# The opening of an attention and MoE kernel: its first mean square summed by TensorE in four chunks, the third weight pair rebased and half decoded earlier, and the first products of v put behind the broadcast

## The chip, the core and the metric

The kernel runs on one core of one Trainium2 chip. The metric is the device time of one execution in microseconds (us), the median of several runs. A profile is one further execution, recorded by the hardware profiler. Its times count from the first instruction that it shows. The engines are TensorE (PE, with its weight loads as PEld), VectorE (DVE), ScalarE (ACT), GpSimd (POOL) and the DMA queue that SyncE feeds (SP). Each engine works through its own list of instructions in order and waits where an operand isn't ready or a buffer isn't free.

## What is computed

Eight sequences of 576 tokens go through local attention with eight heads of 64, then through a gated feed-forward block. The reference, cut to its core:

```python
scores = q @ k.T / sqrt(64)                    # heads 0-3: the last 32 keys; heads 4-7: every 4th of the last 128
attn = softmax(where(mask, scores, -1e9))
x = (attn @ v) with the heads side by side     # 4608 tokens x 512
xn = x / sqrt(mean(x * x, axis=-1) + 1e-6) * rms_g
g, val = xn @ w_gate, xn @ w_val               # 512 -> 1536
out = (g * sigmoid(g) * val) @ w_out           # 1536 -> 512
```

All inputs and the output are float32. The weights arrive as 64-bit words (the float64 form of the values), and the kernel makes float32 of them on the chip.

## The kernel before

**Units.** The 4608 tokens are cut into 16 units of 288 (`U`). A unit's attention comes in 14 blocks: for each of four pairs of heads (`c` = 0 to 3) three or four blocks of 96 or 72 queries. A block goes through five stations: the scores on TensorE (`scored`, tile `s`), the masked maximum on VectorE (`scores_max`, two instructions, tile `t`), the exponential on ScalarE (`scores_exp`), the sum, its reciprocal and the scaling (`scores_norm`), the transposition on TensorE (`transposed`) with its copy `pt` on ScalarE, and the product with the values (`output`, tile `o`) whose copy into `xraw` is made by `take`. Then `square` squares a chunk of `xraw` on ScalarE and, in unit 0 alone, multiplies it by `rms_g` on GpSimd.

**The mean square.** Before, the squares of the four chunks are added to one tile, by GpSimd or VectorE (the function inside `square`), and `rms_sum` makes a column sum of them with six small matmuls against `inv` (1/512 in each element; tile `rps`). `rms_root` adds 1e-6 on VectorE and raises to the power of -1/2 on GpSimd (tile `rst`), `spread_first` multiplies the identity by it on VectorE (tile `rd`), `rms_apply` broadcasts it to all partitions with a matmul against ones (tile `bps`). From there ScalarE copies `root`, and VectorE multiplies the four chunks by it (`normal`, tiles `xn`).

**The feed-forward part.** For each of 12 column blocks `j`, `gate` makes the product g (four matmuls in unit 0), ScalarE its tanh, VectorE the gate `h` from both (`silu`); `val` makes the product v, and VectorE multiplies h by it (`prod`); `proj` multiplies the last h by w_out into four banks `acc`. g and v of successive j take turns in two banks of PSUM, tags "g" and "v" (`bank`): the bank that g of j+1 writes is the one in which v of j lay, so it is free once `prod` has read it. In unit 0 the first g and v (`first`, `start`) are made of the x that isn't normalized yet, by table `FIRST`, and multiplied by `root` later (tiles `g_first` and `h`).

**The weights.** They come in pairs of 128x512 pieces, 18 pairs in all (`load_pieces`, tiles `raw`, three buffers). `rebase` scales a pair's upper words into `f`, pairs 0 to 2 on GpSimd, later ones on ScalarE; from pair 4 on GpSimd also scales the upper words in place. The rest of the decoding is VectorE's: `shift`, `low` and `sign` for pairs 0 to 3, `rest` and `whole` from pair 4 on, and behind the last of them the next pair's load is issued. Pair 0 holds g and v of j = 0, pair 1 of j = 1, pair 2 w_out of j = 0 and g of j = 2, pair 3 v of j = 2 and w_out of j = 1.

**What sets the order.** The order on every engine is written out by a counter of steps (`now`). `later(dt, rank, fn)` puts a piece of work off by `dt` steps; `flush` issues the work of a step sorted by rank; then TensorE's matmuls of that step are issued by `attend`. The first 25 steps (`ends`) are the attention of unit 0. There `STEPS` says how many decode operations each step issues, `REBASES` in which steps a pair is rebased, `FIRST` where the first products stand, `ZEROS` where the upper halves of unit 1's query tiles are cleared, and `BUSY` how many matmuls on ones keep TensorE running (`busy`, five at the start, then two per step, and one in steps 17 to 19). Step 25 on belongs to the loop over `u` and `j`, three steps for a j: in it a step issues one decode operation (`decode`, two in the step `TWICE`, none in the step `PAUSE`), unit 1's blocks go along by table `SCORES`, and `split_weight` cuts the weights into a high and a low part for the later units. Once the last operation of a pair is issued, the next rebase on ScalarE follows (`begun`, `rebase_next`).

Of the kernel before, what the change touches and what calls it, by code (L numbers as in the profile page):

```python
# [9 lines left out]
F32 = mybir.dt.float32  # L10
# [4 lines left out]
ALU = mybir.AluOpType  # L15
# [5 lines left out]
P = 128  # L21
# [4 lines left out]
QB = 96  # L26
# [10 lines left out]
LAG, OUT, LATER = 4, 2, 1  # L37
STEPS = (0,) * 6 + (1, 0, 1, 0, 1) + (0,) * 2 + (1, 0, 0, 0, 1, 1) + (0,) * 4 + (2, 0)
REBASES = 5, 11, 20, 23
BUSY = 5, 2  # L40
SIGNS = 4
# [6 lines left out]
SECOND = 14, 18, 22  # L48
ZEROS = 19, 23, 26
FIRST = {19: (("g", 0), ("g", 1)), 20: (("g", 2),), 22: (("g", 3), ("v", 0), ("v", 1)),  # L50
         23: (("v", 2), ("v", 3))}

# [24 lines left out]
def attn_moe(ctx: ExitStack, tc: tile.TileContext, qk_in, v_in, w_gate, w_val, w_out, rms_g, outT):  # L77
# [82 lines left out]
    def rebase(m):  # L160
        fs[m] = cst.tile([P, 2, NC, P], F32, tag=f"slot{m}", name=f"f_{m}")


        high = raws[m][..., 1].bitcast(F32)
        if m < len(REBASES) - 1:
            G.tensor_scalar(out=fs[m], in0=high, scalar1=2.0 ** -112, scalar2=1.0, op0=ALU.mult, op1=ALU.mult)
        else:
            A.activation(out=fs[m], in_=high, func=AF.Copy, scale=2.0 ** -112)
        if m >= SIGNS:

            G.tensor_scalar(out=high, in0=high, scalar1=0.0, scalar2=1.0, op0=ALU.mult, op1=ALU.mult)
# [45 lines left out]
    def step():  # L217
        if ops:
            m, f = ops.pop(0)
            while state["rebased"] <= m:  # L220
                ahead()
            f(m)
            if (f == low and m == len(REBASES) - 1) or (f == whole and m < NP - 2):
                begun.append(m)
# [219 lines left out]
    def square(u, c):  # L444
        first = c == 0
        sq = sb.tile([P, U], F32, tag="xsq" if first else "tmp", name=f"sq_{u}_{c}", bufs=1 if first else 2)
        x = xraw[u, c]
        A.activation(out=sq, in_=x, func=AF.Square)
        if u == 0:
            G.tensor_scalar(out=x, in0=x, scalar1=gs[:, c:c + 1], scalar2=1.0, op0=ALU.mult, op1=ALU.mult)  # L450
        if first:
            xsq[u] = sq
        else:
            e = V if c == NC - 1 or u == 1 or u == 0 and c > 1 else G
            total = lambda: e.tensor_tensor(out=xsq[u], in0=xsq[u], in1=sq, op=ALU.add)
            if u == 0 and c == NC - 1:
                total()
            else:
                later(1, 0.4 if u or c < 2 else 0.55, total)

# [18 lines left out]
    def products(q, t, o, t_ps, s_tag="s", o_tag="o", wait=0):  # L479
# [50 lines left out]
        if o:  # L530
            if o[0] < NEX or wait:
                later(1, 0.5 if o[0] < NEX else 0.55, lambda: take(*o, o_ps))
            else:
                for a in range(2):
                    later(1, (0.1, 0.3)[a], lambda a=a: take(*o, o_ps, (a,)))
            if o[0] < NEX:
                later(1, 9, lambda: load_v(further(o, 3)))
            far = further(o, 2)
            if far and far[0] >= NEX:
                split_v(far, 8 if o[0] < NEX else 1)  # L540
        if q:
            later(1, 0.7, lambda: scores_max(*q, s_ps))
            behind = q == (1, 0, 2)
# [21 lines left out]
    rst = {}  # L565

    def rms_sum(u):
        r_ps = ps.tile([QB, NB, 2], F32, tag="o", name=f"rps_{u}")
        for i in range(NB):
            PE.matmul(r_ps[:, i, :], xsq[u][:, i * QB:(i + 1) * QB], inv, start=True, stop=True)  # L570
        later(1, 0.1 if u == 1 else -1.2, lambda: rms_root(u, r_ps))
        if u == 0:
            later(1, 6, spread_first)

    def rms_root(u, r_ps):
        r = sb.tile([QB, NB], F32, tag="rst", name=f"rst_{u}", bufs=2)
        V.tensor_scalar(out=r, in0=r_ps[:, :, 0], scalar1=1e-6, scalar2=None, op0=ALU.add)
        G.tensor_tensor(out=r, in0=r, in1=mhalf, op=ALU.pow)
# [91 lines left out]
    def start(kind, c):  # L670

        if kind not in first:
            first[kind] = ps.tile([P, 512], F32, tag={"g": "acc1", "v": "acc3"}[kind], name=f"{kind}_0_0")
        three(first[kind][:, :U], weight(kind, 0, 0), c, xraw[0, c], c == 0, c == NC - 1)
# [104 lines left out]
    busy_ps = ps.tile([P, 512], F32, tag="acc3", name="busy")  # L779

    def busy(n):

        for _ in range(n):
            PE.matmul(busy_ps, ones, ones[:, None, :].to_broadcast([P, 4, P]), start=True, stop=True)

# [4 lines left out]
    def plan(u, base, q_at, t_at, o_at):  # L790
# [25 lines left out]
    for n in range(ends):  # L816
# [118 lines left out]
```

## Time and profile before

| | us |
|---|---|
| median of 3 runs | 1105.61 |
| lowest, highest run | 1105.19, 1106.04 |
| the profiled execution | 1105.86 |
| its span, first to last instruction | 1104.1 |
| TensorE busy | 1095.4 (99%) |
| VectorE busy | 787.5 (71%) |
| ScalarE busy | 613.0 (56%) |
| GpSimd busy | 674.2 (61%) |

A row of the timeline has the start and the duration in us, the engine, the line of the kernel, the operation, output and inputs by the program's names, the shape, and how many instructions are merged into it. In brackets stand the idle time of the engine just ahead of the row and what ended it. [...] The granted TensorE clock is at full speed in all forty slices of the page.

### The profile page before, as it was taken

The numbers are of one execution on the slowest core, as the hardware profiler recorded it, in microseconds if no ns is written. First come the engines' busy times: TensorE is split into PE (matmuls) and PEld (weight loads), VectorE is DVE, ScalarE is ACT, GpSimd is POOL, SyncE is SP. The second block draws the span as 40 slices with busy tenths as digits, with TensorE's granted clock in tenths as the row PEclk, the third lists the DMA queues.
The fourth block names the chain that finished last, engine by engine and source line by source line (L and its number), as shares of the span: only waits on it lengthen the run. The fifth ranks groups of instructions, "written<-read, shape, count | busy, mean of one in ns | idle before, by whom it ended". The sixth has DMA issues, their size and how long they took to land.

```text
span 1104.1 us, 25573 instructions
## 1 busy us (share of the span) xinstructions
PE 1095.4 (99%) x8390; PEld 1069.8 (97%) x8390; DVE 787.5 (71%) x3097; ACT 613.0 (56%) x2200; POOL 674.2 (61%) x1153
## 2 busy tenths in 40 slices
PE   8999999999999999999999999999999999999998
PEld 6787999999999999999999999999999999999998
DVE  7889667868687676877768687686867768687412
ACT  5795676546465564646556464564646556464211
POOL 7433589756586675757657585675758657584211
PEclk9999999999999999999999999999999999999999
DMA  9775212212131131312212131131212212120000
GB/s 255 197 250 182 75 44 87 85 35 82 43 93 53 41 93 34 96 42 62 77 37 85 42 85 52 48 98 29 86 43 80 65 32 82 52 76 14 17 7 22
DMA packets 61543, 82.18 MB, mean 74 GB/s; under 512 B 7298, under 2 KB 41090, under 8 KB 61410
## 3 DMA queue, kind: packets, MB, share of 16 engines
q1 hardware_dynamic: 61410, 80.54, 24.5%
q8 instruction: 67, 1.10, 0.4%
q14 instruction: 66, 0.54, 0.2%
HBM read 71.08 MB, written 9.44 MB: 73 GB/s over the span
## 4 chain that ended last, share of the span: by engine, by line
PE 95%; ACT 1%; DVE 1%; POOL 1%; issue 1%; DMA 1%; SPq 0%; POOLq 0%; ACTq 0%; DVEq 0%
PE acc L666 17%; PE g L666 17%; PE v L666 17%; PE acc L663 9%; PE g L663 9%; PE v L663 9%; PE s L519 3%; PE o L507 3%; PE acc L660 2%; PE v L660 2%; PE g L660 2%; PE t L492 2%; PE g L492 1%; PE o L504 1%; PE s L516 1%
## 5 line engine op out<-in xcount | busy, mean ns | idle before, releaser
L733 POOL TENSOR_TENSOR hlo<-th,hhi 128x288 fp32r<-128x288 f32 x179 | 145.8, 814 | 161.3 <-ACT hhi L732 146.9
L399 ACT ACTIVATE t<-t,sum 96x128 f32<-96x128 f32 (+3 forms) x448 | 165.8, 373 | 108.9 <-DVE sum L384 106.3
L666 PE MATMUL acc<-hhi,lo 128*128 128x288 f32 x720 | 212.7, 295 | 0.0
L415 POOL TENSOR_SCALAR t<-t,sum 72x72 f32<-72x72 f32 (+3 forms) x414 | 147.8, 368 | 85.9 <-DVE sum L409 74.9
L703 ACT ACTIVATE th<-g 128x288 f32<-128x288 f32 x180 | 73.8, 410 | 194.0 <-PE g L666 99.2
L666 PE MATMUL g<-xhi,lo 128*128 128x288 f32 x612 | 180.3, 295 | 0.0
L666 PE MATMUL v<-xhi,lo 128*128 128x288 f32 x612 | 180.2, 294 | 0.0
L437 DVE TENSOR_REDUCE xraw<-o 64x72 f32<-64x144 f32 (+1 forms) x364 | 117.0, 322 | 83.9 <-PE o L507 79.5
L708 DVE SCALAR_TENSOR_TENSOR th<-th,g 128x288 f32<-128x288 f32 x180 | 80.8, 449 | 100.0 <-ACT th L703 76.1
L666 PEld LDWEIGHTS acc<-hhi,lo 128*128 128x128 f32 x720 | 135.4, 188 | 0.0
L323 POOL TENSOR_TENSOR vhl<-vt,vhl 128x128 fp32r<-128x128 f32 x182 | 84.4, 464 | 70.1 <-ACT vhl L319 66.6
L732 ACT CAST hhi<-th 128x288 fp32r<-128x288 f32 x180 | 77.7, 432 | 76.0 <-DVE th L721 75.1
L666 PEld LDWEIGHTS g<-xhi,lo 128*128 128x128 f32 x612 | 115.2, 188 | 0.0
L666 PEld LDWEIGHTS v<-xhi,lo 128*128 128x128 f32 x612 | 115.1, 188 | 0.0
L721 DVE TENSOR_TENSOR th<-th,v 128x288 f32<-128x288 f32 x180 | 79.8, 443 | 43.6 <-PE v L666 43.5
L439 DVE TENSOR_TENSOR xraw<-o,xraw 64x72 f32<-64x72 f32 (+1 forms) x364 | 101.2, 278 | 12.5
L663 PE MATMUL acc<-hhi,hi_o 128*128 128x288 f32 x360 | 109.0, 303 | 0.0
L663 PE MATMUL g<-xhi,hi_g 128*128 128x288 f32 x357 | 107.0, 300 | 0.0
L666 PE MATMUL acc<-hlo,hi_o 128*128 128x288 f32 x360 | 106.4, 296 | 0.0
L362 POOL TENSOR_TENSOR qs<-qk,qs 64x288 fp32r<-64x288 f32 x104 | 84.3, 811 | 24.5 <-ACT qs L357 17.3
L353 POOL TENSOR_TENSOR ks<-qk,ks 128x288 fp32r<-128x288 f32 (+2 forms) x104 | 97.1, 938 | 3.1
L666 PE MATMUL g<-xlo,hi_g 128*128 128x288 f32 x322 | 95.1, 295 | 0.0
(188 smaller groups left out, 3463.4 us busy)
## 6 DMA issues: line engine op xcount, KB each, us to landing
qk<-in_qk_dram SPq DMA_DIRECT2D x60, 288.0 KB, 2.8
vt<-in_v_dram SPq DMA_DIRECT2D x196, 64.0 KB, 1.9
qk<-in_qk_dram SPq DMA_DIRECT2D x30, 352.0 KB, 3.0
out_dram<-ot SPq DMA_DIRECT2D x64, 144.0 KB, 1.9
qk<-in_qk_dram SPq DMA_DIRECT2D x30, 304.0 KB, 2.8
raw<-in_w_gate_dram SPq DMA_DIRECT2D x12, 512.0 KB, 5.4
raw<-in_w_val_dram SPq DMA_DIRECT2D x12, 512.0 KB, 5.5
raw<-in_w_out_dram SPq DMA_DIRECT2D x12, 512.0 KB, 4.4
```

The lines of the kernel that those rows point to most:

```text
L323: G.tensor_tensor(out=vp[:, :, 1], in0=vs.pop(b), in1=vp[:, :, 0], op=ALU.subtract)
L353: ek.tensor_tensor(out=ks[:, 1, :nkt], in0=kr, in1=ks[:, 0, :nkt], op=ALU.subtract)
L362: eq.tensor_tensor(out=qs[D:], in0=qr[D:], in1=qs[D:], op=ALU.subtract)
L399: A.activation(out=t[:nq, a, :n], in_=t[:nq, a, :n], func=AF.Exp, scale=-1.0, bias=sm[:nq, a, 0:1], accum_out=None if by_rows(u, c, i) els ...
L415: (V if u == 0 and (c, i) > (NC - 1, 0) else G).tensor_scalar(out=t[:nq, a, :n], in0=t[:nq, a, :n], scalar1=sm[:nq, a, 3:4], scalar2=1.0, ...
L437: V.tensor_reduce(out=ours, in_=o[:D, cols:cols + 2 * nq].rearrange("d (t q) -> d q t", t=2), axis=mybir.AxisListType.X, op=ALU.add)
L439: V.tensor_tensor(out=ours, in0=o[D:, cols:cols + nq], in1=ours, op=ALU.add)
L663: PE.matmul(out, wh[:, cc, :], xh, start=start, stop=False)
L666: PE.matmul(out, w[:, cc, :], v, start=False, stop=stop and k == 1)
L708: V.scalar_tensor_tensor(out=t, in0=t, scalar=1.0, in1=g, op0=ALU.add, op1=ALU.mult)
L721: V.tensor_tensor(out=t, in0=t, in1=v_ps[:, :U], op=ALU.mult)
L733: (V if (u, j) == (NU - 1, NJ - 1) else G).tensor_tensor(out=lo, in0=t, in1=hi, op=ALU.subtract)
```

## The change

The squares of the four chunks of unit 0 are no longer added. Each chunk's square goes to TensorE by itself as soon as it is there (`part_sum`, six small matmuls each, in steps 12, 13 and 18 by the new table `SUMS` and in step 21), into 24 columns of the bank in which the dummies write. The dummies have 384 columns for that, and there are three per step for two (seven at the start for five), none in the steps with a sum or a first product. VectorE adds up the four sums with one reduction (`rms_root`). Three additions of squares go: one on GpSimd, two on VectorE.

The tables: pair 2 is rebased in step 16, not 20, and its shift and low stand in steps 19 and 20, its sign in step 24; before, shift and low stood in step 23 and the sign in step 25. The rest of the decoding moves up by one operation, and with it ScalarE's rebases from pair 4 on: `begun` is set behind the shift of pair 3, not behind its low. In the first products one chunk of v stands ahead of the broadcast and three behind it, two and two before, and v lies in the bank "acc0". The maxima of unit 1's first scores and the spread change places by rank, the copies of o stand ahead of the exponentials of the same step (rank 0.41), and unit 1's tiles are cleared later.

The diff, cut to its core:

```diff
-STEPS = (0,) * 6 + (1, 0, 1, 0, 1) + (0,) * 2 + (1, 0, 0, 0, 1, 1) + (0,) * 4 + (2, 0)
-REBASES = 5, 11, 20, 23
+STEPS = (0,) * 6 + (1, 0, 1, 0, 1) + (0,) * 2 + (1, 0, 0, 0, 1, 1, 1, 1, 0, 0, 0, 1)
+REBASES = 5, 11, 16, 23
...
-            if (f == low and m == len(REBASES) - 1) or (f == whole and m < NP - 2):
+            if (f == shift and m == len(REBASES) - 1) or (f == whole and m < NP - 2):
...
         if u == 0:
             G.tensor_scalar(out=x, in0=x, scalar1=gs[:, c:c + 1], scalar2=1.0, op0=ALU.mult, op1=ALU.mult)
-        if first:
+        if u == 0:
+            squares.append(sq)
+        elif first:
             xsq[u] = sq
...
-                later(1, 0.5 if o[0] < NEX else 0.55, lambda: take(*o, o_ps))
+                later(1, 0.41 if o[0] < NEX else 0.55, lambda: take(*o, o_ps))
...
-            later(1, 0.7, lambda: scores_max(*q, s_ps))
+            later(2 if q == (1, 0, 0) else 1, 0.6 if q == (1, 0, 0) else 0.7, lambda: scores_max(*q, s_ps))
...
+    def part_sum(c):
+        for i in range(NB):
+            PE.matmul(sum_ps[:, c, i, :], squares[c][:, i * QB:(i + 1) * QB], inv, start=True, stop=True)
+
     def rms_sum(u):
+        if u == 0:
+            part_sum(NC - 1)
+            later(1, -1.2, lambda: rms_root(u, sum_ps))
+            later(1, 0.65, spread_first)
+            return
...
-        V.tensor_scalar(out=r, in0=r_ps[:, :, 0], scalar1=1e-6, scalar2=None, op0=ALU.add)
+        total = r_ps[:, :, 0]
+        if u == 0:
+            V.tensor_reduce(out=r, in_=r_ps[..., 0].rearrange("q c i -> q i c"), axis=mybir.AxisListType.X, op=ALU.add)
+            total = r
+        V.tensor_scalar(out=r, in0=total, scalar1=1e-6, scalar2=None, op0=ALU.add)
...
+    sum_ps = busy_ps[:QB, 3 * P:3 * P + 2 * NB * NC].rearrange("q (c i t) -> q c i t", c=NC, t=2)
...
-            PE.matmul(busy_ps, ones, ones[:, None, :].to_broadcast([P, 4, P]), start=True, stop=True)
+            PE.matmul(busy_ps[:, :3 * P], ones, ones[:, None, :].to_broadcast([P, 3, P]), start=True, stop=True)
...
-        if n < nb + LAG + OUT:
+        if n in SUMS:
+            part_sum(SUMS.index(n))
+        elif n < nb + LAG + OUT and n not in FIRST:
             busy(0 if n < 2 else BUSY[1] if n < nb + LAG - 1 else 1)
```

Where the instructions stand. On TensorE, from the first product on; g_0_0 and v_0_0 are the first products, s_1 are scores of unit 1, a product's second input is the weight pair. Before:

```order
L660 MATMUL g_0_0_528<-xraw_0_0_255,f_0_215 128x288
L660 MATMUL g_0_0_528<-xraw_0_1_329,f_0_215 128x288
L516 MATMUL s_1_0_0_534<-qk_1_0_115 96x128 x2
L660 MATMUL g_0_0_528<-xraw_0_2_411,f_0_215 128x288
L516 MATMUL s_1_0_1_545<-qk_1_0_115 96x128 x2
L570 MATMUL rps_0_556<-inv_73,sq_0_0_334 96x2 x3
L660 MATMUL g_0_0_528<-xraw_0_3_493,f_0_215 128x288
L660 MATMUL v_0_0_561<-xraw_0_0_255,f_0_215 128x288
L660 MATMUL v_0_0_561<-xraw_0_1_329,f_0_215 128x288
L516 MATMUL s_1_0_2_579<-qk_1_0_115 96x128 x2
L612 MATMUL bps_0_582<-rd_0_572,ones32_99 128x288
L660 MATMUL v_0_0_561<-xraw_0_2_411,f_0_215 128x288
```

In the change, at the same place:

```order
L670 MATMUL g_0_0_545<-xraw_0_0_262,f_0_220 128x288
L670 MATMUL g_0_0_545<-xraw_0_1_339,f_0_220 128x288
L515 MATMUL s_1_0_0_550<-qk_1_0_115 96x128 x2
L568 MATMUL busy_146<-inv_73,sq_0_3_553 96x2 x3
L515 MATMUL s_1_0_1_559<-qk_1_0_115 96x128 x2
L670 MATMUL g_0_0_545<-xraw_0_2_424,f_0_220 128x288
L670 MATMUL g_0_0_545<-xraw_0_3_511,f_0_220 128x288
L670 MATMUL v_0_0_583<-xraw_0_0_262,f_0_220 128x288
L515 MATMUL s_1_0_2_591<-qk_1_0_115 96x128 x2
L622 MATMUL bps_0_594<-rd_0_571,ones32_99 128x288
L670 MATMUL v_0_0_583<-xraw_0_1_339,f_0_220 128x288
L670 MATMUL v_0_0_583<-xraw_0_2_424,f_0_220 128x288
```

The sum is the last chunk's alone and stands one product and one block of scores earlier, the products with chunks 2 and 3 follow it together, and one product of v has gone from ahead of bps to behind it.

On ScalarE, from the first tanh (h_0) on; f_4 is the rebase of pair 4, xraw_1_0 the copy of unit 1's first o, rows with a sum as an output are exponentials. Before:

```order
L703 ACTIVATE h_0_608<-g_first_609 128x288
L472 COPY pt_1_0_0_625<-t_0_0_620 128x192
L399 ACTIVATE t_1_0_2_600,sum1_87<-t_1_0_2_600,sum1_87 96x128 x2
L399 ACTIVATE t_1_1_0_612,sum2_88<-t_1_1_0_612,sum2_88 96x128 x2
L412 ACTIVATE t_1_0_2_600<-t_1_0_2_600,sum1_87 96x128 x2
L703 ACTIVATE h_1_650<-g_0_1_636 128x288
L472 COPY pt_1_0_1_652<-g_0_1_636 128x192
L168 ACTIVATE f_4_659<-raw_4_521 128x1024
L412 ACTIVATE t_1_1_0_612<-t_1_1_0_612,sum2_88 96x128 x2
L399 ACTIVATE t_1_1_1_654,sum3_89<-t_1_1_1_654,sum3_89 96x128 x2
L433 COPY xraw_1_0_677<-o_1_0_0_668 64x96 x2
```

In the change, at the same place:

```order
L713 ACTIVATE h_0_624<-g_first_625 128x288
L169 ACTIVATE f_4_633<-raw_4_539 128x1024
L471 COPY pt_1_0_0_644<-t_0_0_639 128x192
L401 ACTIVATE t_1_0_2_613,sum1_87<-t_1_0_2_613,sum1_87 96x128 x2
L401 ACTIVATE t_1_1_0_628,sum2_88<-t_1_1_0_628,sum2_88 96x128 x2
L414 ACTIVATE t_1_0_2_613<-t_1_0_2_613,sum1_87 96x128 x2
L713 ACTIVATE h_1_669<-g_0_1_655 128x288
L471 COPY pt_1_0_1_671<-g_0_1_655 128x192
L414 ACTIVATE t_1_1_0_628<-t_1_1_0_628,sum2_88 96x128 x2
L435 COPY xraw_1_0_694<-o_1_0_0_687 64x96 x2
L401 ACTIVATE t_1_1_1_673,sum3_89<-t_1_1_1_673,sum3_89 96x128 x2
```

The rebase of pair 4 has moved up by six rows, and the copy of o stands ahead of the last exponentials.

On VectorE, up to the product of h_2 with v; raw_4, f_4 are rest and whole of pair 4, raw_5 and f_5 of pair 5, rows with a mask are maxima. Before:

```order
L252 TENSOR_TENSOR lo_0_688<-f_0_215,hi0_g0_687 128x512
L186 SCALAR_TENSOR_TENSOR raw_4_521<-raw_4_521 128x1024
L190 SCALAR_TENSOR_TENSOR f_4_659<-f_4_659,raw_4_521 128x1024
L408 TENSOR_REDUCE sum4_90<-sum4_90 96x2
L409 RECIPROCAL sum4_90<-sum4_90 96x2
L384 ISA t_1_2_0_735,sum0_86<-s_1_2_0_722,mask_77 72x104
L384 ISA sum0_86 72x1
L384 ISA t_1_2_0_735,sum0_86<-s_1_2_0_722,mask_77 72x104
L384 ISA sum0_86 72x1
L708 SCALAR_TENSOR_TENSOR h_2_731<-h_2_731,g_0_2_717 128x288
L186 SCALAR_TENSOR_TENSOR raw_5_617<-raw_5_617 128x1024
L721 TENSOR_TENSOR h_2_731<-h_2_731,v_0_2_743 128x288
```

In the change, the rows up to the same product:

```order
L253 TENSOR_TENSOR lo_0_703<-f_0_220,hi0_g0_702 128x512
L187 SCALAR_TENSOR_TENSOR raw_5_636<-raw_5_636 128x1024
L410 TENSOR_REDUCE sum4_90<-sum4_90 96x2
L411 RECIPROCAL sum4_90<-sum4_90 96x2
L386 ISA t_1_2_0_754,sum0_86<-s_1_2_0_741,mask_77 72x104
L386 ISA sum0_86 72x1
L386 ISA t_1_2_0_754,sum0_86<-s_1_2_0_741,mask_77 72x104
L386 ISA sum0_86 72x1
L718 SCALAR_TENSOR_TENSOR h_2_750<-h_2_750,g_0_2_736 128x288
L191 SCALAR_TENSOR_TENSOR f_5_732<-f_5_732,raw_5_636 128x1024
L731 TENSOR_TENSOR h_2_750<-h_2_750,v_0_2_765 128x288
```

One decode operation more is done ahead of the product: whole of pair 5 stands where its rest stood. It is the same ahead of the product of h_1, where the sign of pair 3 stands for its low.

On VectorE around the root, the four decode operations f_1 low, f_1 sign, f_2 shift and f_2 low follow each other with nothing between, then come the reduction, the addition of 1e-6, the maxima of the first scores and the spread; before, the two additions of squares stood among them, and shift and low of pair 2 came behind the root. The sign of pair 2 now stands ahead of g_first, before it stood behind h_0's gate. On GpSimd the rebase of pair 2 stands between the scalings of chunks 1 and 2, in the place of the addition of squares; before, it stood between those of chunks 2 and 3, behind two clearings of unit 1's tiles. The order of SP's queue changes only from pair 13's load on, around 75 us of the trace before.

More of the change, by code (lines that the diff above doesn't have):

```diff
@@ L37 @@
 LAG, OUT, LATER = 4, 2, 1
-STEPS = (0,) * 6 + (1, 0, 1, 0, 1) + (0,) * 2 + (1, 0, 0, 0, 1, 1) + (0,) * 4 + (2, 0)
-REBASES = 5, 11, 20, 23
-BUSY = 5, 2
+STEPS = (0,) * 6 + (1, 0, 1, 0, 1) + (0,) * 2 + (1, 0, 0, 0, 1, 1, 1, 1, 0, 0, 0, 1)
+REBASES = 5, 11, 16, 23
+BUSY = 7, 3
+SUMS = 12, 13, 18
 SIGNS = 4
@@ L48 @@
 SECOND = 14, 18, 22
-ZEROS = 19, 23, 26
-FIRST = {19: (("g", 0), ("g", 1)), 20: (("g", 2),), 22: (("g", 3), ("v", 0), ("v", 1)),
-         23: (("v", 2), ("v", 3))}
+ZEROS = 22, 24, 26
+FIRST = {19: (("g", 0), ("g", 1)), 21: (("g", 2), ("g", 3)), 22: (("v", 0),),
+         23: (("v", 1), ("v", 2), ("v", 3))}
 SCORES = {1: (-3, -2, 0, 1, 3, 4, 6, 7, 9, 10, 12, 13, 15, 16),
@@ L164, in rebase @@
         high = raws[m][..., 1].bitcast(F32)
-        if m < len(REBASES) - 1:
+        if m < 3:
             G.tensor_scalar(out=fs[m], in0=high, scalar1=2.0 ** -112, scalar2=1.0, op0=ALU.mult, op1=ALU.mult)
@@ L370, in attn_moe @@
     st, xraw, xsq = {}, {}, {}
+    squares = []
     def scores_max(u, c, i, s_ps):
@@ L450, in square @@
             G.tensor_scalar(out=x, in0=x, scalar1=gs[:, c:c + 1], scalar2=1.0, op0=ALU.mult, op1=ALU.mult)
-        if first:
+        if u == 0:
+            squares.append(sq)
+        elif first:
             xsq[u] = sq
         else:
[L454 to L459, printed above, removed]
+            later(1, 0.4, lambda: (V if c == NC - 1 or u == 1 else G).tensor_tensor(out=xsq[u], in0=xsq[u], in1=sq, op=ALU.add))
     def bursts(u):
@@ L571, in rms_sum @@
         later(1, 0.1 if u == 1 else -1.2, lambda: rms_root(u, r_ps))
-        if u == 0:
-            later(1, 6, spread_first)
     def rms_root(u, r_ps):
         r = sb.tile([QB, NB], F32, tag="rst", name=f"rst_{u}", bufs=2)
-        V.tensor_scalar(out=r, in0=r_ps[:, :, 0], scalar1=1e-6, scalar2=None, op0=ALU.add)
+        total = r_ps[:, :, 0]
[3 more added lines that the diff above has]
+        V.tensor_scalar(out=r, in0=total, scalar1=1e-6, scalar2=None, op0=ALU.add)
         G.tensor_tensor(out=r, in0=r, in1=mhalf, op=ALU.pow)
@@ L672, in start @@
         if kind not in first:
-            first[kind] = ps.tile([P, 512], F32, tag={"g": "acc1", "v": "acc3"}[kind], name=f"{kind}_0_0")
+            first[kind] = ps.tile([P, 512], F32, tag={"g": "acc1", "v": "acc0"}[kind], name=f"{kind}_0_0")
         three(first[kind][:, :U], weight(kind, 0, 0), c, xraw[0, c], c == 0, c == NC - 1)
@@ L794, in plan @@
         last = base + (o_at[-1] if u < NNAT else DONE)
-        events.setdefault(last + (4 if u == 1 else 3), {})["sum"] = u
+        events.setdefault(last + (2, 4, 3)[min(u, 2)], {})["sum"] = u
         events.setdefault(last + (4, 7, 5)[min(u, 2)], {})["apply"] = u
@@ L799, in attend @@
         e = events.pop(now[0], {})
+        if e.get("sum") == 0:
+            rms_sum(e.pop("sum"))
         if any(k in e for k in "qto"):
```

## The prediction

> **What bounds the kernel now.** I read the page's first line, then the view of who waited for whom, for TensorE alone and over the whole run, then the timeline of TensorE across the opening; the last line of the fence is a row of the chain of waits.
>
> ```profile
> span 1104.1 us, 25573 instructions
> ...
> PE busy L784 <- ACT ones L94: 2.4, 1, 2.4
> PE o L504 <- ACT xraw L433: 1.5, 2, 1.3
> PE t_first L492 <- POOL t L415: 0.7, 2, 0.5
> PE g L660 <- POOL xraw L450: 0.4, 1, 0.4
> ...
> 29.81 1.13 PE L660 MATMUL g<-xraw,f 128*128 128x288 f32 x4
> 30.78 0.60 PE L516 MATMUL s<-qk 128*96 128x128 f32 x4
> 31.22 0.65 PE L660 MATMUL g<-xraw,f 128*128 128x288 f32 x2
> ...
> 33.15 0.75 PE L660 MATMUL g<-xraw,f 128*128 128x288 f32 x2 [0.41 <-POOL xraw L450]
> ...
> 35.14 0.72 PE L612 MATMUL bps<-rd,ones 96*128 96x288 f32 x2
> 35.70 1.14 PE L660 MATMUL v<-xraw,f 128*128 128x288 f32 x4
> ...
> 37.28 2.13 PE L660 MATMUL g<-xn,f 128*128 128x288 f32 x8
> ...
> 46.11 0.59 PE L504 MATMUL o<-pt,v 128*128 128x192 f32 x2 [1.28 <-ACT xraw L433]
> 46.54 2.10 PE L660 MATMUL g<-xn,f 128*128 128x288 f32 x8
> ...
> 54.13 2.10 PE L660 MATMUL g<-xn,f 128*128 128x288 f32 x8
> ...
> 97.55 0.43 PE rps L570 x6
> ```
>
> The four groups are all the waits that TensorE has in 1104.1 us. Of the second group only 0.2 us is left behind the wait at 46.11; otherwise TensorE runs without a gap to the end, so nothing that makes another engine faster later can shorten the span. What the change wins it must win ahead of the row at 46.54, the product g_0_2, and it keeps that only if no new wait appears behind. What can go is 0.41 us ahead of 33.15, 1.28 us ahead of 46.11, and dummies on the path. Each row begins with its issue; from one start to the next is what it costs its engine.
>
> **The change part by part.** *Dummies and sums.* Six sum matmuls cost 0.43 (last row), a pair of scores 0.44 (30.78 to 31.22), two g matmuls 0.97 (29.81 to 30.78). Ahead of the first products one dummy goes, one becomes a sum and one is shorter; in the earlier steps 1152 dummy columns stand for 1024, and two steps have a sum instead. TensorE waits for other engines between these, so I count the gain at nothing where the sum of columns alone would say 0.3, and keep 0.3 either way.
>
> *The rebase of pair 2, moved ahead on GpSimd.* It stands where an addition of squares stood.
>
> ```profile
> 23.89 1.23 DVE L415 TENSOR_SCALAR t<-t,sum 72x72 f32<-72x72 f32 x2
> 27.11 1.22 DVE L177 SCALAR_TENSOR_TENSOR f<-raw,f 128x1024 uint32<-128x1024 uint32 x1
> 28.25 0.45 DVE L455 TENSOR_TENSOR sq<-sq,sq 128x288 f32<-128x288 f32 x1
> 28.61 1.22 DVE L181 SCALAR_TENSOR_TENSOR f<-raw,f 128x1024 uint32<-128x1024 uint32 x1
> 33.11 0.67 DVE L174 TENSOR_SCALAR f<-f 128x1024 uint32<-128x1024 uint32 x1
> ...
> 24.10 0.79 POOL L455 TENSOR_TENSOR sq<-sq,sq 128x288 f32<-128x288 f32 x1
> 27.99 2.21 POOL L450 TENSOR_SCALAR xraw<-xraw,gs 128x288 f32<-128x288 f32 x1 [3.11 <-ACT sq L448]
> 31.49 1.12 POOL L166 TENSOR_SCALAR f<-raw 128x1024 f32<-128x1024 f32 x1
> 32.58 0.51 POOL L450 TENSOR_SCALAR xraw<-xraw,gs 128x288 f32<-128x288 f32 x1
> 33.05 1.46 POOL L578 TENSOR_TENSOR rst<-rst,mhalf 96x3 f32<-96x3 f32 x1
> 99.14 0.87 POOL L578 TENSOR_TENSOR rst<-rst,mhalf 96x3 f32<-96x3 f32 x1 [1.81 <-DVE rst L577]
> ```
>
> Two small normalizations on VectorE took 1.23 us from 23.89 on: they stood until GpSimd's addition was over at 24.10 + 0.79 = 24.89. GpSimd in turn took 2.21 us for a scaling that takes 0.51 at 32.58: it stood through three VectorE instructions in a row, to 28.61 + 1.22 = 29.83. So each shuts the other out. A rebase of 1.12 where the addition of 0.79 stood makes VectorE's normalizations, and TensorE's transposes behind them, 0.33 later. That I set against the dummies, and let the first product start at 29.81 again.
>
> VectorE then runs four decode steps in one piece: low and sign of pair 1, shift and low of pair 2. A big one costs 1.14 (27.11 to 28.25), a shift 0.6 (its 0.67 less the same overlap): 27.11 + 0.33 + 1.14 + 1.14 + 0.6 + 1.14 = 31.46. By the row at 27.99 GpSimd stands all that time, and its two scalings end at 31.9 and 32.4. TensorE asks for them at 29.81 + 0.97 + 0.44 + 0.43 + 0.44 = 32.09 and 32.57: just in time, and the wait of 0.41 goes. The power on the sums follows at 32.4. It took 1.46 beside the shift at 33.11, and 0.87 at 99.14; no decode step stands beside it now, so 33.3, and the spread (rd, the size of the addition at 28.25, 0.45) is there at 33.75.
>
> TensorE comes to the broadcast (bps) at 32.09 + 0.97 + 0.49 + 0.44 = 33.99, behind rd: no wait, and 35.14 before. Then bps 0.56, three products 1.46, scores 0.44, transposes 0.17 (as before in sum): the first product on the normalized x starts at **36.6, 0.7 us earlier** than 37.28.
>
> [...]
>
> *Behind the broadcast.*
>
> ```profile
> 36.32 1.52 DVE L623 TENSOR_TENSOR xn<-xraw,bps 128x288 f32<-128x288 f32 x4
> 38.31 0.46 DVE L702 TENSOR_TENSOR g_first<-g,root 128x288 f32<-128x288 f32 x1
> 44.81 0.44 DVE L721 TENSOR_TENSOR h<-h,v 128x288 f32<-128x288 f32 x1
> 46.86 0.14 DVE L408 TENSOR_REDUCE sum<-sum 96x2 f32<-96x4 f32 x1
> ...
> 47.12 0.67 DVE L252 TENSOR_TENSOR lo<-f,hi_g 128x512 fp32r<-128x512 f32 x1
> 51.87 1.23 DVE L186 SCALAR_TENSOR_TENSOR raw<-raw 128x1024 uint32<-128x1024 uint32 x1 [0.70 <-POOL raw L171]
> 53.01 0.45 DVE L721 TENSOR_TENSOR h<-h,v 128x288 f32<-128x288 f32 x1
> 55.15 1.34 DVE L252 TENSOR_TENSOR lo<-f,hi_g 128x512 fp32r<-128x512 f32 x1
> ...
> 38.80 0.44 ACT L703 ACTIVATE h<-g_first 128x288 f32<-128x288 f32 x1
> 52.88 1.17 ACT L168 ACTIVATE f<-raw 128x1024 f32<-128x1024 f32 x1
> ...
> 54.13 1.83 POOL L171 TENSOR_SCALAR raw<-raw 128x1024 f32<-128x1024 f32 x1 [2.30 <-ACT f L168]
> ```
>
> From xn's end (37.84) to g_first (38.31) VectorE has one block's maxima, 0.47; a sum with its reciprocal costs 0.26 (46.86 to 47.12); an instruction on 128x288 costs 0.36 (28.25 to 28.61). Ahead of xn VectorE now takes the second block's maxima and, once ScalarE has its two exponentials (at most 0.44 each, the tanh's row being longer), its sum: 33.75 + 0.47 + 0.85 + 0.26 = 35.3, against 36.32. But the sign of pair 2 (1.14) now stands ahead of g_first, which it followed before: 35.3 + 1.52 + 0.47 + 1.14 = 38.4 where 38.31 stood. The tanh is 0.49 behind that, at 38.8 to 38.9. Of xn's 1.0 us nothing is left here.
>
> ScalarE now rebases pair 4 (1.17, by 52.88) right behind that tanh, no longer ahead of the copy of o that TensorE waited for at 46.11; the exponentials ahead of that copy go behind it, too. What is left ahead is a scaling that waits for VectorE's second sum, 43.5 below, and two small ones: the copy is done by 44.6. TensorE asks at 36.6 + 7.55 (37.28 to 46.11 without the wait) = 44.2: **the wait of 1.28 shrinks to some 0.4**.
>
> *What is late next.* The bank that g_0_2 writes is free when VectorE has multiplied h_1 with v. That ended at 44.81 + 0.37 = 45.18, in time for 46.54 less 1.28. In the changed order one more decode step (sign of pair 3) stands ahead of it. From the tanh at 38.8: gate 39.2, shift 39.6, product 40.2, h times root 40.5. Meanwhile ScalarE's rebase ends at 40.4, and GpSimd's scaling of pair 4 (1.12) starts beside the product, which reads PSUM. h times root has both operands in SBUF, as the subtraction at 55.15 has, which took 1.34 against 0.67 at 47.12 while GpSimd's scaling of 54.13 ran to 55.96. So h times root ends at 41.8. Undisturbed, the sum behind it would still wait for ScalarE's exponentials, to 41.1. From there sum 0.26, low 1.14, sum 0.26 (43.5), maxima 0.47, gate 0.36, sign 1.14, product 0.36 make 4.0: 45.8, or 45.1. TensorE wants g_0_2 at 44.6. So g_0_2 starts at **45.8 (or 45.1), 0.7 (or 1.4) us earlier** than before, held by VectorE.
>
> The next product, h_2 with v, began 8.2 us after that one (44.81 to 53.01) with four big decode steps between and a wait of 0.70 for GpSimd's scaling of pair 5. In the changed order there are four again and the same scaling, behind a longer piece of VectorE's; I leave 8.2. It ends at 54.0 (or 53.3) and frees g_0_3's bank, which TensorE took at 54.13, 0.75 behind the product: there **0.1 (or 0.8)** of the gain is left. I take 0.3, nearer to the disturbed end, which has a row. Further on the order within a j is as before, and 0.3 is less than the 0.75 of cover in the row that was tightest in the opening, so I carry it to the end.
>
> *A second wait, just hidden.* Pair 6's rebase moves one step ahead on ScalarE, ahead of a copy of o, while its load still waits for the sign of pair 3.
>
> ```profile
> 47.00 0.33 SPq L154 DMA_DIRECT2D raw<-in_w_val_dram  x1
> ...
> DMA to landing us min/median/max: 3.2/5.2/7.8
> ```
>
> The loads issue at 45.4 and 45.8 now. Before, the rebase at 52.88 came 5.9 behind 47.00 without a wait, so the pair has landed by 51.3; rebase 1.17 and 1.0 of scaling and copy make 53.5 where TensorE asks at 45.8 + 7.2 = 53.0. g_0_3 behind it would start at 53.9, and the product holds it to 54.0 anyway.
>
> **Sum.** The profiled execution took 1105.86 us, the span of 1104.1 and 1.8 around it; less 0.3 it is 1105.6. It stands 0.25 above the median of the runs, 1105.61, whose forecast is **1105.3**. A measurement of this kernel can tell some 0.2% (2.2 us) from no change.
>
> **Rivals.** *TensorE's own order is the bound.* If VectorE's products are never late, 0.7 + 1.28 stays: 1103.6. For it speaks that I add many small pieces; against it that 0.75 us of cover was left at 53.38 and the gain must fit in. Chance 0.20.
>
> *The broadcast doesn't come earlier, against what the change says.* If GpSimd is shut out over 1.1 us longer than reckoned, bps stays at 35.1 while the sign of pair 2 now delays g_first: VectorE's chain is 1.2 later than above and g_0_3 starts at 55.2, 1.1 late: 1106.7. The 2.21 row speaks for it; against it, VectorE has little to run behind 31.46. Chance 0.14.
>
> *Slower: ScalarE stands at pair 6's rebase.* At the longest landing, 7.8 us, the load is there at 53.6, the copy done at 55.8, g_0_3 starts at 56.2, 2.1 late: 1107.7. It decides from a landing of 5.6 us on. Chance 0.10.
>
> **How the numbers follow.** The forecast has 0.56, with a range of its own from 1104.8 (0.8 gained) to 1105.5. The range goes down to the first rival and up to the second, 1103.6 to 1106.7; outside lie the third and the tails. Faster by over 0.2% needs more than all waits named: 0.06. Slower by over 0.2% needs the longest landing and a little: 0.06. Within: 0.88.
>
> **What will show it.** Right: no wait ahead of the last g_0_0 product, bps near 34.0, the first product on xn near 36.6, and in TensorE's list of waits a VectorE product (h from h and v) ahead of g where the copy of o stood. Wrong: TensorE without any wait from 37 to 60; a wait for a copy of o near 53; bps at 35 or later; the wait of 1.28 still there.

## The result, and the profile after

The changed kernel is slower. The median of its nine runs is 1111.83 us, beside 1105.86 for nine runs of the kernel before on the same chip: a ratio of 1.0053, 95% interval 1.0034 to 1.0073. The forecast was 1105.3 with a range up to 1106.7, so the time lies outside it, and on the other side.

The single runs say more than the median, because they come in steps, and the steps go with TensorE's mean granted clock: 1107.56 and 1107.59 at a clock of 1.000, 1109.12 at 0.998, 1110.98 at 0.997, 1111.83 at 0.995, and 1114.11 to 1114.86 at 0.992. The kernel before had 1.000 in the profile that the prediction read. So there are two losses: some **1.7 us at full clock** (1107.57 against 1105.86), and **0 to 7 us that come with the clock**, in the median run 4.3. Two single executions far off all others, 1514 us of run 8 and 3778 us of the kernel before, are left out of every median and count below.

The profiled execution is the run of 1110.98, its span 1109.2 against 1104.1. The view of who waited for whom, for TensorE (engine, tile and line; what it waited for; us in total, times, longest):

```profile
PE busy L796 <- ACT ones L95: 2.4, 1, 2.4
PE s L515 <- DVE sum L386: 1.4, 1, 1.4
PE t_first L491 <- POOL t L417: 1.3, 2, 0.9
PE v L670 <- ACT pt L471: 0.6, 1, 0.6
PE t_first L491 <- DVE t L417: 0.3, 1, 0.3
PE o L503 <- ACT xraw L435: 0.2, 1, 0.2
PE bps L622 <- ACT rd L606: 0.2, 1, 0.2
```

The two waits that the prediction wanted gone are gone: nothing waits for a GpSimd scaling ahead of g, and the 1.28 us for the copy of o is gone (the 0.2 is the second wait of that group, there before). In their place stand 1.4 us for VectorE's maxima (s, the scores) and 0.6 us for a copy of pt (v, a value product), and the transposes t_first wait 1.6 us in the opening where they waited 0.7. All waits together are 6.4 us where they were 5.0: 1.4 of the 5.1 us that the span grew. The rest is in no list of waits. It is in the granted clock, which the windows view shows; its columns are the stretch and its length, TensorE's busy time with its instructions, the granted clock, the share of the DMA engines and GB/s:

```profile
core 0: us, PE busy (x), PEclk, DMA share, GB/s
30.50:31.00 0.50, 0.50 (x5) 1.00 0.46 101
31.00:31.50 0.50, 0.50 (x3) 0.57 0.12 33
...
37.00:37.50 0.50, 0.50 (x3) 0.50 1.09 173
37.50:38.00 0.50, 0.50 (x3) 0.61 0.77 109
```

In the rows not shown the clock is 1.00 or 0.50 and nothing between, so a half microsecond at 0.57 was at full clock for 14% of it: the clock fell at 31.07, and by the row at 0.61 it rose at 37.89. That is 6.8 us at half clock, 3.4 us lost, which is what lies between this run and those at 1.000, and, with the 1.4 of waits, nearly all that the span grew. TensorE's busy time doesn't show it: it is 0.50 of 0.50 throughout. What shows it is the timeline, where the same instructions take nearly twice as long:

```profile
21.28 0.77 PE L796 MATMUL busy<-ones 128*128 128x384 f32 x3
...
22.70 0.61 PE L568 MATMUL busy<-inv,sq 128*96 128x2 f32 x6
...
24.03 0.61 PE L568 MATMUL busy<-inv,sq 128*96 128x2 f32 x6
...
25.01 0.79 PE L796 MATMUL busy<-ones 128*128 128x384 f32 x3
...
30.69 1.95 PE L670 MATMUL g<-xraw,f 128*128 128x288 f32 x4
...
35.10 2.13 PE L670 MATMUL g<-xraw,f 128*128 128x288 f32 x4
...
38.38 0.65 PE L622 MATMUL bps<-rd,ones 96*128 96x288 f32 x2
```

The first four matmuls of g (two products, each with two matmuls in the profile) took 1.13 us in the kernel before; here they take 1.95, as the clock falls 0.38 us behind their start, and the next four, at half clock throughout, take 2.13. The broadcast starts at 38.38, where 33.99 was forecast, and ahead of that, between the dummies that end at 21.89 and those at 25.01, TensorE had 3.1 us of small products only: transposes, scores and value products on 72 columns, and the sums, which stand where dummies stood.

### The profile page after: what moved, and what is told of

The parts are those of the page before. It is cut to its first block, busy times and chain, and to the rows that moved or that the text cites. A ratio compares the mean times of both kernels' runs of the same rounds, so it can differ in the third digit from the quotient of the medians.

```text
span 1109.2 us, 25625 instructions
## 1 busy us (share of the span) xinstructions
PE 1099.1 (99%) x8417; PEld 1074.8 (97%) x8417; DVE 783.1 (71%) x3096; ACT 613.6 (55%) x2200; POOL 670.4 (60%) x1152
## 4 chain that ended last, share of the span: by engine, by line
PE 92%; DVE 2%; POOL 2%; ACT 2%; DMA 1%; issue 1%; SPq 0%; POOLq 0%; DVEq 0%; ACTq 0%
PE acc L676 17%; PE v L676 17%; PE g L676 17%; PE acc L673 9%; PE v L673 9%; PE g L673 8%; PE o L506 3%; PE s L518 3%; PE t L491 2%; PE g L670 1%; PE acc L670 1%; PE v L670 1%; PE s L515 1%; PE g L491 1%; DMA raw<-in_w_val_dram 1%
```

## The experiments

Three theories for the clock: **C**, the dummies that the sums displaced; **W**, TensorE's new short waits; **D**, the dummies' 384 columns in place of 512. For the 1.7 us at full clock: **V**, the decode that runs one step ahead, against **S**, the sums themselves. "The clock fell" below means a mean clock of 0.998 or less; as an estimate, that is at least some 3.3 us at half clock in a span of 1105 (0.998 is rounded from 0.9985 at most, 0.15% of the span is 1.66 us, and at half clock half of the time is lost). A mean of 0.999 isn't counted: in the profile of the kernel before the clock goes down behind TensorE's last product as well, where nothing is lost. That product's row is at 1100.42, and between 1103.5 and 1104.0 the clock is 0.87 with TensorE busy for 0.00 us. Each group of four ran on one chip beside runs of the kernel before, whose medians were 1105.59, 1105.80 and 1105.81.

### 1. All dummies back

```diff
         if n in SUMS:
             part_sum(SUMS.index(n))
-        elif n < nb + LAG + OUT and n not in FIRST:
+        if n < nb + LAG + OUT:
             busy(...)
```

> The changed kernel, with the dummies of steps 12, 13, 18 and 19 issued besides the sums. Theory C (clock): the dummies taken out where the sums stand let the granted clock fall to half for a time that differs from run to run, 0 to 7 us lost. Then all runs here have a clock of 1.000 and lie close together, at 1107.6 (the changed kernel's best runs) plus up to 1.9 for the dummies' own time on TensorE: 1107.6 to 1109.5, no run above 1110. Rival W (waits): the clock falls because TensorE waits (0.94 at 13.63, 0.35 at 26.14), which this edit leaves: runs still spread up to 1114 with clocks down to 0.992. Rival D (narrow dummies): the clock falls because the dummies have 384 columns in place of 512: still spread, too.

Measured: 1108.41 to 1108.90 in six runs, clock 0.999 to 1.000 in all; ratio 1.0028 (1.0017 to 1.0040). The steps are gone. The dummies are still the narrow ones, so D falls, and the waits of 0.7 and 1.4 us behind the opening are there, too. W isn't settled by this run: the wait of 0.35 at 26.14 is gone from its profile, too, as the dummies fill it. The loss at full clock stays.

### 2. The kernel before without four steps' dummies

```diff
-        if n < nb + LAG + OUT:
+        if n < nb + LAG + OUT and n not in (12, 13, 18, 19):
             busy(...)
```

> The kernel before, without the dummies of steps 12, 13, 18 and 19 (two, two, one and one), and nothing else changed; no part of the result is left out. Theory C: the clock falls below 1.000 in some or all runs, with times from 1105.3 to 1113. Rival W and rival D: clock 1.000 in all runs and 1105.0 to 1106.0, since the waits and the width of the other dummies are those of before.

Measured: median 1107.52 (1105.53 to 1108.42), ratio 1.0015 (1.0006 to 1.0023); the clock fell in 8 of 11 runs, to 0.995. So taking the dummies away does it without anything else of the change. The profile is of a run at full clock, so it doesn't show where the clock fell in the others.

### 3. The changed kernel with the old decode

```diff
-STEPS = (0,) * 6 + (1, 0, 1, 0, 1) + (0,) * 2 + (1, 0, 0, 0, 1, 1, 1, 1, 0, 0, 0, 1)
-REBASES = 5, 11, 16, 23
+STEPS = (0,) * 6 + (1, 0, 1, 0, 1) + (0,) * 2 + (1, 0, 0, 0, 1, 1) + (0,) * 4 + (2, 0)
+REBASES = 5, 11, 20, 23
...
-            if (f == shift and m == len(REBASES) - 1) or (f == whole and m < NP - 2):
+            if (f == low and m == len(REBASES) - 1) or (f == whole and m < NP - 2):
```

> The changed kernel with the decode steps and the rebase of the third pair where they were before. Theory C: the clock falls as in the changed kernel (0.992 to 1.000, a spread of several us). For the 1.7 us that the changed kernel's best runs lose at full clock: theory V (VectorE and GpSimd collisions from the moved decode) says that the best runs here come back to 1105 to 1106.3; rival S (the sums and the order of the products cost it) says that they stay at 1107 to 1108.

Measured: 1104.78 to 1105.86 in the four runs at clock 1.000, and up to 1114.92 (clock 0.989) in the others; ratio 1.0026 (1.0006 to 1.0045). At full clock the loss of 1.7 is gone: theory V. The parts of the edit go together here; runs 7, 8 and 11 separate the opening from what comes behind it. The profile is of a run at 0.997, and it speaks plainly on the clock. The windows view, with the columns as above:

```profile
26.00:28.00 2.00, 2.00 (x20) 1.00 1.01 193
28.00:30.00 2.00, 2.00 (x17) 0.82 0.87 171
30.00:32.00 2.00, 2.00 (x10) 0.50 0.96 276
```

TensorE was busy 2.00 of 2.00 in each of these, and in the three stretches ahead of them from 20 on; its timeline names no idle time from 22 to 60. So no wait in the 9 us ahead of the fall lowered this clock, and W falls as the cause here: a TensorE that by its records never rests can still lose its clock. Half clock isn't always paid in full either: this run had 6.8 us of it, 3.4 us lost by the sum above, and its 1106.58 is only 0.7 to 1.8 us above the four at full clock.

### 4. The kernel before with the new decode

The same lines the other way round, in the kernel before.

> The kernel before with only the rebase and decode steps of the third pair moved ahead. Theory C: clock 1.000 in all runs, for all dummies are there. Theory V: 1107 to 1108, the 1.7 us that the changed kernel loses at full clock. Rival S: within 0.5 of the kernel before, 1105.3 to 1106.4.

Measured: 1110.71 to 1112.01 in five runs, clock 0.995 to 0.997 in all; ratio 1.0052 (1.0040 to 1.0064). I had expected a full clock, since no dummy is missing. None of the five is at full clock, so the times say nothing of V against S; but the list of waits has, with no sums by chunks in the kernel, the two that V needs:

```profile
PE s L516 <- DVE sum L384: 1.4, 1, 1.4
PE v L660 <- ACT pt L472: 1.1, 1, 1.1
```

The timeline has a long wait ahead of the fall; VectorE, GpSimd, then TensorE, and the windows:

```profile
23.64 2.30 DVE L415 TENSOR_SCALAR t<-t,sum 72x72 f32<-72x72 f32 x2
...
23.86 0.80 POOL L455 TENSOR_TENSOR sq<-sq,sq 128x288 f32<-128x288 f32 x1
24.64 1.09 POOL L166 TENSOR_SCALAR f<-raw 128x1024 f32<-128x1024 f32 x1
...
25.92 0.33 PE L492 MATMUL t_first<-ident,t 72*72 72x72 f32 x2 [1.09 <-DVE t L415]
...
24.00:26.00 2.00, 0.91 (x8) 1.00 1.03 152
26.00:28.00 2.00, 2.00 (x14) 0.70 1.04 222
```

In this kernel GpSimd has the addition of squares and the rebase, and VectorE's two normalizations stand through both: 2.30 us. TensorE waits 1.09 and was busy 0.91 of 2.00 us between 24 and 26; the clock fell at 26.8, by the row at 0.70. So theory W isn't wrong everywhere: a long wait in the opening goes with a lower clock, too, though no run here took that wait away alone. In the changed kernel, which has no addition there, the wait is 0.35, and run 3, which has none, loses its clock as well.

### 5 and 6. Which dummies: the late two steps or the early two

Both stand on run 3, the changed kernel with the old decode, which has no waits of its own.

```diff
-        elif n < nb + LAG + OUT and n not in FIRST:
+        if n < nb + LAG + OUT and n not in (12, 13):      # run 5
+        if n < nb + LAG + OUT and n not in (18, 19):      # run 6
```

> The changed kernel with the old places of the third pair's decode, and the dummies of steps 18 and 19 back, those of 12 and 13 left out. Theory L (late): the clock falls because the last steps ahead of the first products have small products only; in both profiles of kernels without those dummies it fell 0.4 to 0.7 us behind the first product's start. Then clock 1.000 in all runs, 1105.2 to 1106.2 (1105.5, the full-clock runs without the dummies, and up to 0.7 for these). Theory E (early): steps 12 and 13 count as much; the clock still falls in about half of the runs, up to 1115.

> The counterpart of the run before: the dummies of steps 12 and 13 back, those of 18 and 19 left out. Theory L: the clock still falls in half of the runs, 1105.5 to 1112. Theory E: clock 1.000, 1105.5 to 1106.8.

Measured: with the late dummies (5) the clock still fell in 5 of 12 runs, to 0.992; 1105.68 to 1113.10, ratio 1.0014 (1.0001 to 1.0027). With the early ones (6) it was 1.000 in all 11; 1106.49 to 1107.73, ratio 1.0008 (1.0000 to 1.0017). My theory L fell (and the fall in the two profiles that it named came 0.38 and 0.34 us behind the first product's start, 31.07 after 30.69 and 29.27 after 28.93, not 0.4 to 0.7). **The dummies of steps 12 and 13 hold the clock**, the two steps in which the sums displaced the dummies in the middle of small transposes and scores. Whether it is their place or their number isn't shown: run 6 gives back six dummies, three in each step, and run 5 two, one in each. Run 6 is also 1.4 us above the kernel before in its median, over the range expected, with a wait of 0.64 for a copy of o in its profile; the old decode isn't free of waits once these dummies are back. The profile of run 5 has the fall where this says it should be, right behind those steps. The timeline, then the windows:

```profile
21.79 0.62 PE L568 MATMUL busy<-inv,sq 128*96 128x2 f32 x6
23.12 0.61 PE L568 MATMUL busy<-inv,sq 128*96 128x2 f32 x6
24.09 0.98 PE L796 MATMUL busy<-ones 128*128 128x384 f32 x3
```

```profile
24.00:24.50 0.50, 0.50 (x6) 1.00 1.11 201
24.50:25.00 0.50, 0.50 (x5) 0.51 0.99 167
...
41.50:42.00 0.50, 0.50 (x4) 0.92 0.00 0
```

From 24.51 to 41.58 it stayed at half: 17.1 us.

### 7 and 8. The wait for pt and the wait for the maxima

On run 1, with all dummies. Run 7 has the first line, run 8 both.

```diff
-            if (f == shift and m == len(REBASES) - 1) or (f == whole and m < NP - 2):
+            if (f == low and m == len(REBASES) - 1) or (f == whole and m < NP - 2):
...
-                    decode((t != PAUSE) + (t == TWICE))
+                    decode((t not in (2, PAUSE)) + (t == TWICE))
```

> The changed kernel with all four steps' dummies back (1108.7 at full clock), and in it ScalarE's rebase of the fifth pair one step later again: behind the fourth pair's low part, as before, and no longer behind its shift. The wait of 0.65 for pt ahead of a value product goes. Theory P (waits add up): 1108.0. Theory Q (VectorE's decode, one step ahead, sets the scores' maxima, for which TensorE waits 1.38 at 53.3): TensorE only comes earlier to that wait, which grows to about 2.0, and the time stays at 1108.5 to 1108.8.

> As the run before, and the decode besides pauses for one step behind the opening, so that from there on every decode step stands where it stood in the kernel before; only the third pair's sign stays ahead of the gate. Theory Q: both waits (0.65 and 1.38) go, 1106.4 to 1107.0. Rival R: the moved work in the opening is what costs, and the time stays above 1108.

Measured: run 7 median 1108.14 (1107.30 to 1109.96), ratio 1.0020 (1.0011 to 1.0029): the wait of 0.7 for pt is gone, that of 1.38 for the maxima stands at the same size, and doesn't grow, as Q had it. Against the kernel before on its own chip run 7 loses 2.3 us and run 1 lost 3.1, 0.8 less, about the wait of 0.7, which speaks for P. The clock fell in 1 of 10 runs (0.998). Run 8 median 1105.84 (1105.51 to 1112.01), ratio 1.0006 (0.9995 to 1.0017), the clock down in 1 of 11 (0.995): with the decode put back to its old steps behind the opening, both waits are gone and so is the loss. That is below the range expected. Rival R is out: what was moved ahead in the opening costs nothing that can be measured; what costs is that every later decode step then also comes one step ahead.

### 9 to 12. The early dummies alone, and what is left

Run 9 is the changed kernel with the dummies of steps 12 and 13 alone. Run 10 adds `PAUSE, TWICE = 31, 5` (before 31, 6); run 11 instead adds both lines of run 8; run 12 is run 11 with one dummy in steps 12 and 13 in place of three.

> The changed kernel with the dummies of steps 12 and 13 alone back, beside the sums there. Theory E (these two steps hold the clock): clock 1.000 in all runs and 1107.4 to 1108.4, that is, what the changed kernel takes in its runs at full clock (1107.6) and at most 0.7 more. Rival: with the new decode order TensorE has short waits in the opening, which the old order doesn't have, and the clock still falls in some runs (1109 to 1114).

> As the run before, with the one step that decodes two pieces also put one step earlier, so that the rest of pair 5 no longer stands in the same step as the whole of pair 4. Theory Q2: this order alone makes VectorE wait for GpSimd's scaling of pair 5 and TensorE for the maxima behind it (1.38); that wait goes, the one of 0.65 for pt stays, and the time is 1.0 to 1.4 below the run before, 1106.3 to 1107.0. Rival: the pieces only queue up elsewhere, within 0.4 of the run before.

> The changed kernel with the dummies of steps 12 and 13 back, the fifth pair's rebase behind the low part, and the decode paused for one step behind the opening: sums by chunks, third pair's sign ahead, no new wait. If the waits and the clock are the whole loss, this is within 0.6 of the kernel before on either side, and its best runs 0.3 to 0.6 below it, 1104.9 to 1105.9. If the sums or the moved sign cost something of their own: 1106.3 or more.

> As the run before with one dummy in steps 12 and 13 in place of three each. If the clock asks for no more than a little dense work between the small products: clock 1.000 and up to 0.8 less than the run before. If it goes by the amount of dense work: the clock falls in some runs, up to 1112.

Measured: run 9 median 1108.65 (1107.93 to 1109.80), ratio 1.0026 (1.0017 to 1.0034), the clock fell in 1 of 11 runs (0.998): the two steps' dummies hold the clock with the new decode, too; the median is some 0.3 us over the range expected. Run 10 median 1108.61, ratio 1.0027 (1.0018 to 1.0036), the clock down in 1 of 11 (0.995): no gain, the wait for the maxima is 1.5; Q2 fell, it isn't the double step but the order as a whole. Run 11 median 1105.91, ratio 1.0002 (0.9994 to 1.0011), the clock down to 0.997 in 2 of 11. Run 12: eight of 11 runs between 1104.58 and 1105.51 at full clock, three with the clock down and 1108.22 to 1111.44; ratio 1.0003 (0.9989 to 1.0016). Against run 11's 2 of 11, 3 of 11 doesn't tell whether one dummy a step is too little. None of them beats the kernel before by more than can be measured.

Run 9 is the changed kernel's own order at full clock, and so shows the waits undisturbed. Two rows of its list of waits, then the timelines of TensorE, VectorE and ScalarE:

```profile
PE s L515 <- DVE sum L386: 1.7, 2, 1.4
PE v L670 <- ACT pt L471: 0.7, 1, 0.7
```

```profile
34.73 0.68 PE L515 MATMUL s<-qk 128*96 128x128 f32 x4 [0.34 <-DVE sum L386]
35.24 0.65 PE L622 MATMUL bps<-rd,ones 96*128 96x288 f32 x2
...
41.21 2.21 PE L670 MATMUL v<-xn,f 128*128 128x288 f32 x8 [0.68 <-ACT pt L471]
...
52.95 0.58 PE L515 MATMUL s<-qk 128*72 128x104 f32 x4 [1.39 <-DVE sum L386]
...
55.85 2.10 PE L670 MATMUL g<-xn,f 128*128 128x288 f32 x8
...
41.37 1.17 DVE L733 TENSOR_TENSOR h<-h,root 128x288 f32<-128x288 f32 x1
...
51.05 1.23 DVE L187 SCALAR_TENSOR_TENSOR raw<-raw 128x1024 uint32<-128x1024 uint32 x1 [1.02 <-POOL raw L172]
...
52.63 0.26 DVE L386 CUSTOM_DVE_ANT_0 t<-s,mask 72x104 f32<-72x104 f32 x1
...
39.79 1.16 ACT L169 ACTIVATE f<-raw 128x1024 f32<-128x1024 f32 x1
40.85 0.30 ACT L471 COPY pt<-t 128x192 f32<-128x192 f32 x1
```

ScalarE's rebase of the fifth pair at 39.79 stands ahead of the copy of pt, which TensorE asks for 0.68 us too early. And at 51.05 VectorE waits 1.02 us for GpSimd's scaling of the next pair, with the maxima at 52.63 queued behind it, for which TensorE's scores wait 1.39. In the kernel before, the same wait for GpSimd stood at 51.87 *behind* the maxima of that block, where TensorE didn't feel it, and in run 11 it stands there again. The maxima of the kernel before, then run 11's maxima, its wait, and its g_0_3:

```profile
50.53 0.26 DVE L384 CUSTOM_DVE_ANT_0 t<-s,mask 72x104 f32<-72x104 f32 x1
...
50.26 0.26 DVE L386 CUSTOM_DVE_ANT_0 t<-s,mask 72x104 f32<-72x104 f32 x1
...
51.56 1.23 DVE L187 SCALAR_TENSOR_TENSOR raw<-raw 128x1024 uint32<-128x1024 uint32 x1 [0.67 <-POOL raw L172]
...
53.48 2.10 PE L670 MATMUL g<-xn,f 128*128 128x288 f32 x8
```

In run 11, with the decode one step later, g_0_3 starts at 53.48 from a first product at 30.36, against 55.85 from 30.30 in run 9: 2.4 us, and the medians of runs 9 and 11 differ by 2.7.

## Why the prediction was wrong, step by step

**Dummies and sums: the step that failed.** "TensorE waits for other engines between these, so I count the gain at nothing where the sum of columns alone would say 0.3, and keep 0.3 either way." I priced the displaced dummies by their time on TensorE, a few tenths, and let their absence cost nothing. But the clock went with them. In runs 1 and 6 to 11, which have all dummies of steps 12 and 13, it fell in 6 of 71 executions; in the changed kernel and runs 2, 3 and 5, which have none there, in 25 of 41. (Run 4 has them all and fell in 5 of 5, behind its wait of 1.09 us.) That is 4.3 us of the median run's 6.0. I had the granted clock in front of me, 1.00 in every stretch of the profile of before, and took it as given. Nobody reads what the dummies write, and that should have made me ask what they hold up. No rival of mine had this mechanism.

**The rebase of pair 2 on GpSimd: right.** VectorE's normalizations took 1.53 from 24.64, 0.30 more than before (forecast 0.33).

**GpSimd shut out by four decode steps: wrong, but without effect.** In the changed kernel a scaling issued at 29.04 took 0.71 us and ran behind the first of them, low at 28.16 with 1.22, while sign at 29.41 took 1.41; in run 9 it took 1.54 from 28.67, through one of them. So it stood for the rest of one instruction and not for the piece. The two rows of the changed kernel:

```profile
29.04 0.71 POOL L452 TENSOR_SCALAR xraw<-xraw,gs 128x288 f32<-128x288 f32 x1 [3.09 <-ACT sq L450]
...
29.41 1.41 DVE L182 SCALAR_TENSOR_TENSOR f<-raw,f 128x1024 uint32<-128x1024 uint32 x1
```

My reading, made from the one row of 2.21 us, doesn't agree with these rows. Why that scaling stood through three isn't explained by any run. The wait of 0.41 ahead of the last g_0_0 went, as forecast. The spread is at 33.80 in run 9 (forecast 33.75), but the broadcast at 35.24, not 33.99. What I missed is a scores product ahead of it, which waits 0.34 for the maxima that VectorE does behind the spread; and the first product starts at 30.30, not 29.81. So the broadcast doesn't come earlier (35.14 before), and the first product on the normalized x starts at 37.79, where 36.6 was forecast and 37.28 stood. The rival with that outcome had a chance of 0.14, by another reason.

**The tanh later, h times root disturbed: right.** The instruction that GpSimd's scaling collides with took 1.17 in run 9 against 0.46 in the kernel before, ending at 42.5 (forecast 41.8). The product ahead of it, which reads PSUM, took 0.45 from 40.89 in run 9, with the scaling beside it from 41.10.

**The wait of 1.28 for the copy of o: gone** (forecast: some 0.4 left). But that ScalarE rebases pair 4 right behind the tanh I followed only to the copy of o; the copy of pt stands behind the same rebase and TensorE asks for it first. 0.7 us, not in the sum.

**h_2·v 8.2 later: right in size, wrong in what it holds; this step failed, too.** In run 9 it starts 8.28 us behind h_1·v (54.31 and 46.03). But I took g_0_3's bank for the only thing that waits for VectorE there. The maxima stand in the same piece, now behind the wait for GpSimd, and TensorE's scores, four rows ahead of g_0_3, stop 1.39 us for them. I had quoted the wait of 0.70 and asked only how long the piece takes, not which of its instructions someone waits for. The wait of this step and that of the one above are 2.1 us together, against 1.7 us lost at full clock, and g_0_3 starts 1.7 us later in run 9 than in the kernel before (55.85 and 54.13), where 0.3 earlier was forecast; run 11 has neither, and is back at the time of the kernel before.

**The second wait, pair 6's load: no.** ScalarE's rebase waited 0.24 us for it in the changed kernel; nothing came of it.

**The chances.** Slower by over 0.2% had 0.06. The steps were reckoned to tenths of a microsecond, while the clock can move the time by 7 us; the range came only from the terms that I had written down.

## What to carry to other kernels

Matmuls whose result nobody reads may be what holds TensorE's clock (here it fell in 6 of 71 executions of runs 1 and 6 to 11, with those of steps 12 and 13, and in 25 of 41 without them): before you displace them, look at how long the stretch of small products becomes without them (here 3.1 us), and give that a rival of its own, with half clock for some 7 to 17 us, as in the profiles here. When a chain is moved one step ahead, look, for each instruction in it that can wait, at what is queued behind it on its engine, and not only when the chain ends: the same wait of 0.7 to 1.0 us cost nothing behind the maxima and 1.4 us ahead of them. And look at single runs, not only at the median: steps in the times name a cause that the list of waits can't show.

## What the runs showed of the hardware

**In four profiles half clock lasted 6.8 to 17.1 us.** It stood from 31.07 to 37.89 in the changed kernel (6.82), 24.51 to 41.58 in run 5 (17.07), and, by the rows below, 29.27 to 36.10 in run 3 (6.83) and 26.79 to 37.03 in run 4 (10.24). The four lengths are close to 2, 5, 2 and 3 times one length of 3.41 us, which is an estimate from these four alone: no profile shows a stretch as short as that. Run 3's rows, then run 4's:

```profile
29.00:29.50 0.50, 0.50 (x2) 0.77 0.74 145
36.00:36.50 0.50, 0.50 (x4) 0.90 0.71 187
...
26.50:27.00 0.50, 0.50 (x4) 0.79 1.09 212
37.00:37.50 0.50, 0.50 (x7) 0.97 0.61 152
```

**What the clock goes by isn't the busy time of the records.** In run 3 TensorE was busy in all of the 9 us ahead of the fall; in run 2 it was busy 0.31 us of 2.00, between 32 and 34, and the clock stayed:

```profile
32.00:34.00 2.00, 0.31 (x4) 0.23 (x4) 1.31 (x8) 1.95 (x7) 2.00 (x3) 1.00 1.02 340
```

(TensorE, its weight loads, VectorE, ScalarE and GpSimd, then the clock.) With all dummies of steps 12 and 13 (runs 1 and 6 to 11) the clock fell in 6 of 71 executions, with one in each step in 3 of 11, with none in 25 of 41. The kernel before lost it in 5 of its 87 runs beside the experiments, one in the second group of four and four in the third.

**What stays open.** In the changed kernel and in run 3 the clock fell at 31.1 and 29.3, 5 to 6 us behind the stretch without dummies, and in run 5 right at its end. A stretch near the first products was as poor in run 6, without any fall, so it alone isn't enough. Whether the clock goes by the number or the place of the dummies, and over how long a stretch, these runs don't settle.
